# Four reading orders for the 512 tokens that stream through the paired gate and up products

## The chip, the core and the metric

The kernel runs on one core of a Trainium2 chip. The metric is device time in microseconds (us), the median over runs; for one execution there is also a hardware profile. Engines: TensorE (PE, with its weight loads shown as PEld), VectorE (DVE), ScalarE (ACT), GpSimd (POOL), and SyncE (SP), whose queue issues the transfers.

## The reference

One transformer block on 2048 tokens of width 448: sliding-window attention, then a gated feed-forward part, each after a layer norm and with a residual. The change is in the feed-forward part.

```python
def _B_ref(x, w_gate, w_up, w_down):
    g = jnp.einsum("bsd,df->bsf", x, w_gate)      # 448 -> 1792
    u = jnp.einsum("bsd,df->bsf", x, w_up)        # 448 -> 1792
    h = _gelu(g) * u
    return jnp.einsum("bsf,fd->bsd", h, w_down)   # 1792 -> 448
...
h = x + _A_ref(_layernorm(x, axis=-1), A_wqkv, A_wo)
h2 = h + _B_ref(_layernorm(h, axis=-1), B_w_gate, B_w_up, B_w_down)
```

All tensors are float32.

## The kernel before, in words

Every float32 operand of the large products is kept as a high and a low part, and each product is a sum of matmuls over pairs of parts (the list `TERMS`, 11 of them for the width of 448). `xT` holds the normalised activations transposed: partitions are the width, and the 2048 tokens lie one after another along the free axis.

The feed-forward part is cut into 56 products, numbered `n`. One product takes 128 of the 1792 hidden columns for one chunk `c` of 512 tokens: `g` and `u` of size 128 x 512 in two PSUM banks, then Gelu of `g` times `u`, then the down product, which adds to four banks of 128 tokens x 448. Products 0 to 3 are computed with all 128 rows of the array. Products from `PAIRED = 4` on are *paired*: a matmul over 128 rows is split into two over 64 rows each, issued one after the other by the helper `pair` (line 903 of the profile) with the tile positions 0 and 64; one of them adds to the bank of `g` while the other adds to the bank of `u`. In a first phase (10 pairs) the upper half serves `g`, in a second (11 pairs) the halves are swapped. The moving operand of each is `xT[HALF[x], xb, toks]`, 512 tokens of one chunk; for the last term of the upper half it is a copy in `rec[2]` (named `xh`).

The bank pair of a product is fixed by the parity of `n`, so the product after next writes the same banks. The order on PE is written out by hand at the end of `feed_forward`: first phase of product m, first half of the down product of m - 2, second phase of product m, second half of the down product of m - 2. All other engines' instructions are placed by a list scheduler (`Lists.run`) that goes by estimated costs, which the change leaves as they are.

After a product, five instructions turn its banks into the operand of the down product: the Gelu on ACT (line 965) reads the first bank through `src(0)` and writes `g2`; the multiply on DVE (line 967) reads the second bank through `src(1)` and `g2`; ACT makes the high part and DVE the low part (lines 328 and 331); the tiny copies of line 909 only mark that a bank has been finished. At the end of a group of products, line 998 adds the four banks of the down product to the residual `hres`, and in the last group line 1001 sends it out. The last product's down product is issued unpaired at line 992.

Of the kernel before, what the change touches and what calls it, by code (L numbers as in the profile page):

```python
# [11 lines left out]
AF = mybir.ActivationFunctionType  # L12
OP = mybir.AluOpType
# [39 lines left out]
PAIRED = 4  # L53
# [11 lines left out]
def mm(n):  # L65
    return max(n / 2400 + 0.0155, 0.115)
# [154 lines left out]
def block_kernel(ctx: ExitStack, tc, x, wqk_in, wv_in, wo_in, ffn_in, out):  # L221
    nc = tc.nc
# [3 lines left out]
    op = L.op  # L226
# [38 lines left out]
    bank = [psum.tile([128, 512], F32, name=f"bank{i}") for i in range(8)]  # L265
# [32 lines left out]
    def span(name, lo, n):  # L298
        return (name, lo, lo + n)
# [21 lines left out]
    def HR(t):  # L321
        return span("h", t, 1)
# [4 lines left out]
    def to_hi(dst, src):  # L327
        nc.scalar.activation(dst, src, AF.Copy)  # L328

    def to_lo(dst, src, hi, eng=None):  # L330
        (eng or nc.vector).tensor_sub(dst, src, f(hi))  # L331

    def dma(key, size, fn, r=(), w=(), cost=0.44, after=()):
        return op("sp", cost, 0, key, fn, r, w, size=size, after=after)
# [473 lines left out]
    def blocks(m):  # L808
        return m.rearrange("p (b n) -> p b n", b=4)
# [86 lines left out]
    down_a, down_b, phase, whole = {}, {}, {}, []  # L896
    HALF = (slice(0, 64), slice(64, 128))

    def pair(key, n, lat, a, b, r, banks):

        def go():
            for x, (bk, w, m, start, stop) in enumerate((a(), b())):
                nc.tensor.matmul(bank[bk.k][:, 0:n], w, m, start=bool(start), stop=bool(stop),  # L903
                                 tile_position=(64 * x, 0), skip_group_check=True)
        return op("pe", mm(n), lat, key, go, r, (), banks)

    def seen(key, b):

        op("act", 0.08, 0.17, key, lambda: nc.scalar.activation(word[0:1, 0:1], bank[b.k][0:1, 0:1], AF.Copy), (),  # L909
           (), b)  # L910

    def product(n, i, c, k, gn, gi, down):
        get, rat, _ = RECS[i % NR]
        key = FFN + 30 * n
        toks = slice(c * 512, (c + 1) * 512)
        early = n < EARLY
        paired = n >= PAIRED
        bs = []
        for q in range(0 if paired else 2):

            turn = 2 * (n - EARLY) + q + (2 if n == 2 else -2)
            b = Bank("early") if early else Bank(("ffn", turn))
            if not early:
                row[turn] = b
            bs.append(b)
            for a, (h, wb, xb) in enumerate(TERMS):
                whole.append(op("pe", mm(512), 0.403, key + (SWAP if n == 3 else 0) + q * NP + a / NP, lambda a=a, h=h, wb=wb, xb=xb, q=q, b=b: nc.tensor.matmul(  # L927
                    bank[b.k], get()[0][q][h][:, wb, :], xT[:, xb, toks], start=(a == 0), stop=(a == NP - 1)),
                   [span("xT", 4 * c, 4), *rat[q][h]], (), b, tag="early" if early else None))
        if paired:  # L930
            bs = [Bank(("fix", 2 * ((n + 1) % 2) + q)) for q in range(2)]
            phase[n] = [[], []]
            for ph in range(2):


                todo = TERMS if ph else TERMS[:-1]
                for a, (h, wb, xb) in enumerate(todo):
                    def side(x, a=a, h=h, wb=wb, xb=xb, ph=ph, todo=todo):
                        q = x ^ ph
                        m = rec[2][64:128, toks] if x and a == NP - 1 else xT[HALF[x], xb, toks]  # L940
                        return (bs[q], get()[0][q][h][HALF[x], wb, :], m, not ph and a == 0, ph and a == len(todo) - 1)
                    need = [span("xT", 4 * c, 4), *rat[0][h], *rat[1][h]] + ([("xh", c)] if a == NP - 1 else [])
                    phase[n][ph].append(pair(key + 11 * ph + a / NP, 512, 0.403, lambda side=side: side(0),
                                             lambda side=side: side(1), need, bs))
                if not ph:
                    seen(key + 11, bs[1])
        raw = [v_m[:, 1024 * n + 512 * q:1024 * n + 512 * q + 512] for q in range(2 * early)]
        held = [[span("vm", 1024 * n + 512 * q, 512)] if early else [] for q in range(2)]
        for q, b in enumerate(bs if early else ()):
            op("act", 0.49, 0.605, 16 * NB - 20, lambda q=q, b=b: nc.scalar.activation(raw[q], bank[b.k], AF.Copy), (),  # L950
               held[q], b)
        bs = [None, None] if early else bs
        m, o = GH[n % 2]
        at = [span("proj", o + 512 * h, 512) for h in range(2)]

        def gh(h):
            return blocks(m[:, o + 512 * h:o + 512 * h + 512])

        def src(q):
            return blocks(raw[q] if early else bank[bs[q].k])  # L960


        g2, G2 = (raw[0], held[0]) if early else (ge, ["ge"])
        table = 0 if n else 1.29
        op("act", 0.485 + table, 0.608 + table, key + NP, lambda: nc.scalar.activation(  # L965
            blocks(g2), src(0), AF.Gelu_apprx_tanh), held[0], G2, bs[0], after=exps)
        op("dve", 0.605, 0.702, key + 2 * NP, lambda: nc.vector.tensor_tensor(  # L967
            blocks(g2), src(1), blocks(g2), op=OP.mult), [*G2, *held[1]], G2, bs[1], port=early)
        op("act", 0.52, 0.635, key + 2 * NP, lambda: to_hi(gh(0), blocks(g2)), G2, [at[0]])
        op("dve", 0.6, 0.7, key + 2 * NP, lambda: to_lo(gh(1), blocks(g2), gh(0)), [*G2, at[0]], [at[1]], port=True)  # L970

        down_a[n], down_b[n] = [], []
        PARTS = ((0, 0), (1, 0), (0, 1))
        last = n == 4 * NF - 1
        for ph in range(0 if last else 2):
            for j in range(2):
                for a, (oh, wh) in enumerate(PARTS):
                    def side(x, a=a, oh=oh, wh=wh, ph=ph, j=j):  # L980
                        q = 2 * j + (x ^ ph ^ k % 2)
                        return (down[q], gh(oh)[HALF[x], q, :], get()[0][2][wh][HALF[x]], not ph and k == 0 and a == 0,
                                ph and k == gn - 1 and a == 2)
                    (down_b if ph else down_a)[n].append(pair(
                        key + 2 * NP + 6 * ph + 3 * j + a, D, 0.38, lambda side=side: side(0), lambda side=side: side(1),
                        [at[oh], *rat[2][wh]], [down[2 * j], down[2 * j + 1]]))
                if not ph:
                    seen(key + 2 * NP + 3 * j + 3, down[2 * j + 1 - k % 2])

        for a, q in ((0, 0), (0, 1), (2, 0), (2, 1), (1, 0), (1, 1), *((a, q) for q in (2, 3) for a in range(3))) if last else ():  # L990
            oh, wh = PARTS[a]
            down_b[n].append(op("pe", mm(D), 0.38, key + 2 * NP + 3 * q + a, lambda a=a, oh=oh, wh=wh, q=q: nc.tensor.matmul(
                bank[down[q].k][:, 0:D], gh(oh)[:, q, :], get()[0][2][wh], start=False, stop=(a == (1 if q < 2 else 2)),
                skip_group_check=True), [at[oh], *rat[2][wh]], (), down[q]))
        if k == gn - 1:
            for q in range(4):
                t = 4 * c + q
                op("dve", 0.533, 0.626, key + 2 * NP + 3 * q + 3, lambda t=t, b=down[q]: nc.vector.tensor_tensor(  # L998
                    hres[:, t, :], bank[b.k][:, 0:D], hres[:, t, :], op=OP.add), [HR(t)], [HR(t)], down[q])
                if gi == len(GROUPS) - 1:  # L1000
                    dma(key + 40, 224, lambda t=t: nc.sync.dma_start(outr[t * 128:(t + 1) * 128, :], hres[:, t, :]),
                        [HR(t)], ())


    exps = []
# [148 lines left out]
```

## Time and profile before

| what | value |
|---|---|
| median of 2 runs | 734.53 us (734.46 to 734.6) |
| the profiled execution's own time | 734.23 us |
| its span, first to last instruction | 732.5 us |
| mean granted TensorE clock | 0.999 |
| PE busy | 723.8 us (99%) |
| DVE, ACT, POOL busy | 395.9, 365.8, 160.3 us |
| chain that ended last, by engine | PE 93%, ACT 2%, DVE 2%, DMA 1% |

A profile describes one execution; the shares of the chain tell where the end of the run was decided, the busy shares only how full an engine was. A row of the groups reads: line, engine, operation, output from inputs, shape and count, then busy us and mean ns of one, then the engine's idle time before such instructions and what ended it. Matmuls are pipelined, so the mean ns of one matmul is longer than the distance from one start to the next.

### The profile page before, as it was taken

The numbers are of one execution on the slowest core, as the hardware profiler recorded it, in microseconds if no ns is written. First come the engines' busy times: TensorE is split into PE (matmuls) and PEld (weight loads), VectorE is DVE, ScalarE is ACT, GpSimd is POOL, SyncE is SP. The second block draws the span as 40 slices with busy tenths as digits, with TensorE's granted clock in tenths as the row PEclk, the third lists the DMA queues.
The fourth block names the chain that finished last, engine by engine and source line by source line (L and its number), as shares of the span: only waits on it lengthen the run. The fifth ranks groups of instructions, "written<-read, shape, count | busy, mean of one in ns | idle before, by whom it ended". The sixth has DMA issues, their size and how long they took to land.

```text
span 732.5 us, 15381 instructions
## 1 busy us (share of the span) xinstructions
PE 723.8 (99%) x5893; PEld 604.6 (83%) x5893; DVE 395.9 (54%) x1057; ACT 365.8 (50%) x930; POOL 160.3 (22%) x253
## 2 busy tenths in 40 slices
PE   8999999999999999999999999999999999999997
PEld 7887888788888787768888888888888888888886
DVE  7977876776677788748554223144223243233223
ACT  7668776667666888876553222243222233222221
POOL 5615343343344547462000000000000000000000
PEclk9999999999999999999999999999999999999999
DMA  8888445755565777514652000012100000001012
GB/s 285 260 280 248 146 148 179 202 178 156 162 201 160 191 229 206 147 36 102 153 174 88 1 2 1 1 43 84 43 1 2 1 1 2 1 1 52 11 42 101
DMA packets 83138, 79.12 MB, mean 108 GB/s; under 512 B 34104, under 2 KB 72952, under 8 KB 83064
## 3 DMA queue, kind: packets, MB, share of 16 engines
q1 hardware_dynamic: 83064, 78.14, 35.3%
q8 instruction: 46, 0.75, 0.4%
q14 instruction: 28, 0.23, 0.1%
HBM read 48.23 MB, written 29.36 MB: 106 GB/s over the span
## 4 chain that ended last, share of the span: by engine, by line
PE 93%; ACT 2%; DVE 2%; DMA 1%; issue 1%; POOL 0%; SPq 0%; DVEq 0%; ACTq 0%; POOLq 0%
PE bank L903 52%; PE bank L580 9%; PE bank L701 6%; PE bank L629 6%; PE bank L735 6%; PE bank L535 5%; PE bank L779 5%; PE bank L927 2%; PE bank L383 1%; ACT pp L705 1%; DVE mt L633 1%; ACT xT L328 0%; DVE hres L782 0%; DMA hres<-in_x_dram 0%; PE bank L660 0%
## 5 line engine op out<-in xcount | busy, mean ns | idle before, releaser
L633 DVE CUSTOM_DVE_ANT_0 mt<-bank,mt 128x384 bf16<-128x384 f32 (+2 forms) x256 | 127.5, 524 | 38.2 <-PE bank L629 36.4
L705 ACT ACTIVATE pp<-bank 128x384 f32<-128x384 f32 (+2 forms) x352 | 121.5, 388 | 52.4 <-PE bank L701 46.5
L967 DVE TENSOR_TENSOR mt<-bank,mt 128x512 f32<-128x512 f32 x54 | 37.1, 688 | 139.5 <-ACT mt L965 139.5
L716 POOL TENSOR_SCALAR_AFFINE_SELECT pp<-pp 128x512 f32<-128x512 f32 x120 | 75.5, 642 | 124.8 <-ACT pp L705 115.0
L580 PE MATMUL bank<-xT,proj 128*128 128x512 f32 x308 | 101.2, 402 | 0.0
L701 PE MATMUL bank<-rq,rk 104*128 104x384 f32 (+2 forms) x352 | 96.8, 305 | 0.9 <-ACT pp L705 0.6
L965 ACT ACTIVATE mt<-bank 128x512 f32<-128x512 f32 x54 | 32.2, 596 | 113.5 <-PE bank L903 113.5
L629 PE MATMUL bank<-rk,rq 84*128 84x384 f32 (+2 forms) x256 | 82.7, 344 | 0.1
L903 PE MATMUL bank<-xT,rec 64*128 64x512 f32 x656 | 82.0, 388 | 0.0
L903 PE MATMUL bank<-xT,rk 64*128 64x512 f32 x656 | 82.0, 388 | 0.0
L701 PEld LDWEIGHTS bank<-rq,rk 104*128 104x128 f32 x352 | 64.7, 189 | 19.3 <-ACT pp L705 4.8
L903 PEld LDWEIGHTS bank<-xT,rec 64*128 64x128 f32 x656 | 63.0, 184 | 12.2
L903 PEld LDWEIGHTS bank<-xT,rk 64*128 64x128 f32 x656 | 63.0, 184 | 12.2
L998 DVE TENSOR_TENSOR hres<-bank,hres 128x448 f32<-128x448 f32 x64 | 35.5, 616 | 66.1 <-PE bank L903 63.9
L328 ACT ACTIVATE proj<-mt 128x512 fp32r<-128x512 f32 x54 | 34.1, 631 | 71.8 <-DVE mt L967 52.5
L903 PE MATMUL bank<-xT,proj 64*128 64x512 f32 x533 | 66.7, 388 | 0.0
L909 ACT ACTIVATE word<-bank 1x1 f32<-1x1 f32 x162 | 25.6, 158 | 79.2 <-PE bank L903 78.6
L580 PEld LDWEIGHTS bank<-xT,proj 128*128 128x128 f32 x308 | 55.9, 190 | 6.0 <-issue 0.8
L535 PE MATMUL bank<-proj,xT 128*128 128x224 f32 x352 | 60.2, 278 | 0.1
L903 PEld LDWEIGHTS bank<-xT,proj 64*128 64x128 f32 x533 | 51.1, 184 | 10.1 <-ACT word L909 0.3
L331 DVE TENSOR_TENSOR proj<-mt,proj 128x512 fp32r<-128x512 f32 x54 | 37.3, 691 | 36.8 <-ACT proj L328 28.5
L535 PEld LDWEIGHTS bank<-proj,xT 128*128 128x128 f32 x352 | 53.0, 191 | 1.8 <-DVE hres L782 0.3
(117 smaller groups left out, 1106.6 us busy)
## 6 DMA issues: line engine op xcount, KB each, us to landing
rk<-k SPq DMA_DIRECT2D x44, 336.0 KB
rq<-q SPq DMA_DIRECT2D x32, 336.0 KB
q<-proj SPq DMA_DIRECT2D x15, 448.0 KB
raw<-in_ffn_dram SPq DMA_DIRECT2D x7, 736.0 KB
v<-in_ffn_dram SPq DMA_DIRECT2D x7, 736.0 KB
k<-proj SPq DMA_DIRECT2D x11, 448.0 KB
hres<-in_x_dram SPq DMA_DIRECT2D x16, 224.0 KB
out_dram<-hres SPq DMA_DIRECT2D x16, 224.0 KB
```

The lines of the kernel that those rows point to most:

```text
L331: (eng or nc.vector).tensor_sub(dst, src, f(hi))
L535: op("pe", mm(224), 0.29, key + a / 16, lambda a=a, h=h, wb=wb, xb=xb: nc.tensor.matmul(bank[b.k][:, 0:224], xT[:, xb, t * 128:(t + 1) * 1 ...
L580: op("pe", mm(512) + 0.002, 0.403, key, lambda a=a, h=h, wb=wb, xb=xb: nc.tensor.matmul(bank[b.k], wqk[i][:, h, wb, :], xT[:, xb, c * 512: ...
L629: nc.tensor.matmul(bank[b.k][:, o:384], rq[u][0:3 * DH, j, i * 128:i * 128 + 128], rk[u][0:3 * DH, j, m0 * 128:(i + 3) * 128], start=True, ...
L633: nc.vector.tensor_tensor_reduce(junk[s % 2][:, o:384], bank[b.k][:, o:384], mask[:, o:384], 1.0, -BIG, OP.add, OP.max, mx[i // 2][:, i % ...
L701: nc.tensor.matmul(bank[b.k][:, 0:n], rk[u][0:104, j, m * 128:m * 128 + 128], rq[u][0:104, j, lo * 128:(hi + 1) * 128], start=True, stop=True)
L705: nc.scalar.activation(pp[:, j, o * 128:o * 128 + n], bank[b.k][:, 0:n], AF.Exp, scale=SCALE)
L716: nc.gpsimd.affine_select(a, a, pattern=[[0, 4], [-cm, 128]], compare_op=op_, fill=0.0, base=0, channel_multiplier=cm)
L735: nc.tensor.matmul(bank[b.k][32 * j:32 * j + DH + 1, lo * 128:(hi + 1) * 128], v[:, 4 * c - 2 + m, g % 2, j, :], pp[:, j, at[m] * 128:(at[ ...
L779: op("pe", mm(D), 0.38, wk, lambda a=a, h=h, oh=oh, wh=wh, i=i, k=k: nc.tensor.matmul(bank[k.k][:, 0:D], ohl[:, h, oh, i * 128:(i + 1) * 1 ...
L903: nc.tensor.matmul(bank[bk.k][:, 0:n], w, m, start=bool(start), stop=bool(stop), tile_position=(64 * x, 0), skip_group_check=True)
L967: op("dve", 0.605, 0.702, key + 2 * NP, lambda: nc.vector.tensor_tensor(blocks(g2), src(1), blocks(g2), op=OP.mult), [*G2, *held[1]], G2, ...
```

## The change

For the paired products, the 512 tokens are read in an order that depends on `n % 4`. Order 0 is the stored one. Order 1 takes tokens 0, 256, 1, 257 and so on. Order 2 takes tokens 0, 32, 64 to 480, then 1, 33 and so on. Order 3 takes 16 tokens from the first half, 16 from the second, and so on. Output columns are still written to the bank one after another, so the columns of a bank stand in the order in which the tokens were read. The Gelu and the multiply read the bank with the inverse order, so that `g2` and all that follows have the tokens in their usual places. With order 1 their reads of the bank have a step of 2 elements, with order 2 a step of 16, with order 3 they go by runs of 16. Products 0 to 3 and the down products are as before.

```diff
+    READ = [None, ("p (h t) -> p t h", dict(h=2)), ("p (h t) -> p t h", dict(h=16)),
+            ("p (h k l) -> p k h l", dict(h=2, l=16))]
+    BACKW = [("p (b t) -> p b t", dict(b=4)), ("p (t h) -> p h t", dict(h=2)), ("p (t h) -> p h t", dict(h=16)),
+             ("p (k h l) -> p h k l", dict(h=2, l=16))]
+    PLAIN = [("p (b t) -> p b t", dict(b=4)), ("p (h t) -> p h t", dict(h=2)), ("p (h t) -> p h t", dict(h=16)),
+             ("p (h k l) -> p h k l", dict(h=2, l=16))]
+    SAME = [None, ("p (t h) -> p t h", dict(h=2)), ("p (t h) -> p t h", dict(h=16)),
+            ("p (k h l) -> p k h l", dict(h=2, l=16))]
+    def seen_as(ap, how):
+        return ap if how is None else ap.rearrange(how[0], **how[1])
-    def pair(key, n, lat, a, b, r, banks):
+    def pair(key, n, lat, a, b, r, banks, order=None):
         def go():
             for x, (bk, w, m, start, stop) in enumerate((a(), b())):
-                nc.tensor.matmul(bank[bk.k][:, 0:n], w, m, start=bool(start), stop=bool(stop),
+                o = bank[bk.k][:, 0:n]
+                if order is not None:
+                    o, m = seen_as(o, SAME[order]), seen_as(m, READ[order])
+                nc.tensor.matmul(o, w, m, start=bool(start), stop=bool(stop),
                                  tile_position=(64 * x, 0), skip_group_check=True)
...
+        way = n % 4 if n >= PAIRED else 0
...
-                                             lambda side=side: side(1), need, bs))
+                                             lambda side=side: side(1), need, bs, way))
...
-            return blocks(raw[q] if early else bank[bs[q].k])
+            return seen_as(raw[q] if early else bank[bs[q].k], BACKW[way])
...
-            blocks(g2), src(0), AF.Gelu_apprx_tanh), held[0], G2, bs[0], after=exps)
+            seen_as(g2, PLAIN[way]), src(0), AF.Gelu_apprx_tanh), held[0], G2, bs[0], after=exps)
...
-            blocks(g2), src(1), blocks(g2), op=OP.mult), [*G2, *held[1]], G2, bs[1], port=early)
+            seen_as(g2, PLAIN[way]), src(1), seen_as(g2, PLAIN[way]), op=OP.mult), [*G2, *held[1]], G2, bs[1], port=early)
```

## The prediction

> **What bounds the kernel now.** I read the head of the page first, then the chain of waits, then what TensorE (PE) waited for.
>
> ```profile
> span 732.5 us, 15381 instructions
> PE 723.8 (99%) x5893; PEld 604.6 (83%) x5893; DVE 395.9 (54%) x1057; ACT 365.8 (50%) x930; POOL 160.3 (22%) x253
> PEclk9999999999999999999999999999999999999999
> PE bank L903 52%; PE bank L580 9%; PE bank L701 6%; PE bank L629 6%; PE bank L735 6%; PE bank L535 5%; PE bank L779 5%; PE bank L927 2%; PE bank L383 1%; ACT pp L705 1%; DVE mt L633 1%; ACT xT L328 0%; DVE hres L782 0%; DMA hres<-in_x_dram 0%; PE bank L660 0%
> 346.57 379.30 PE bank L903 x3462
> PE bank L903 <- ACT word L909: 0.2, 1, 0.2
> ```
>
> PE is busy for 99% of the span at full granted clock, so there is no clock to win. Line 903 is the helper `pair`, which issues every paired matmul. From 346.57 us the chain lies on it for 379.30 us without a break, and the last row says that in the whole run it waited once, for 0.2 us, on another engine. So in the second half of the kernel a nanosecond added to a paired matmul is a nanosecond of the end. This is the half that the change touches.
>
> Next, how much of it the change touches. The groups by shape give the matmuls of the gate and up products: 64 rows by 512 tokens.
>
> ```profile
> L903 PE MATMUL bank<-xT,rec 64*128 64x512 f32 x656 | 82.0, 388 | 0.0
> L903 PE MATMUL bank<-xT,rk 64*128 64x512 f32 x656 | 82.0, 388 | 0.0
> L903 PE MATMUL bank<-xT,proj 64*128 64x512 f32 x533 | 66.7, 388 | 0.0
> L903 PE MATMUL bank<-xT,rq 64*128 64x512 f32 x287 | 35.9, 388 | 0.0
> L903 PE MATMUL bank<-xh,rk 64*128 64x512 f32 x16 | 6.2, 386 | 0.0
> L903 PE MATMUL bank<-xh,rec 64*128 64x512 f32 x16 | 6.2, 386 | 0.0
> L903 PE MATMUL bank<-xh,proj 64*128 64x512 f32 x13 | 5.0, 386 | 0.0
> L903 PE MATMUL bank<-xh,rq 64*128 64x512 f32 x7 | 2.7, 386 | 0.0
> ```
>
> The counts add up to 2184 matmuls, that is 1092 pairs; at 10 + 11 = 21 pairs for each product these are the 52 paired products, numbers 4 to 55. Thirteen products fall to each of the four orders, or 273 pairs. The mean of 388 ns is a latency that overlaps its neighbours. What a pair costs the path is read from starts, in one product of the timeline (start us, length us):
>
> ```profile
> 600.39 2.45 PE L903 MATMUL bank<-xT,rk 64*128 64x512 f32 x20
> 602.68 1.38 PE L903 MATMUL bank<-proj 64*128 64x448 f32 x12
> 603.89 2.67 PE L903 MATMUL bank<-xT,rk 64*128 64x512 f32 x21
> ...
> 606.40 1.37 PE L903 MATMUL bank<-proj 64*128 64x448 f32 x12
> 606.61 0.60 ACT L965 ACTIVATE mt<-bank 128x512 f32<-128x512 f32 x1 [2.29 <-PE bank L903]
> 607.24 0.69 DVE L967 TENSOR_TENSOR mt<-bank,mt 128x512 f32<-128x512 f32 x1 [3.35 <-ACT mt L965]
> ...
> 607.62 0.62 PE L903 MATMUL bank<-xT,proj 64*128 64x512 f32 x4
> ```
>
> Ten pairs of 512 tokens take 602.68 - 600.39 = 2.29 us and eleven take 606.40 - 603.89 = 2.51 us: 4.80 / 21 = 229 ns a pair. Twelve pairs of 448 columns take 1.21 + 1.22 = 2.43 us: 202.5 ns a pair. The difference, 26 ns for 64 columns, is 0.41 ns per column. So of the 229 ns some 209 ns (512 x 0.41) are the streaming of tokens, and 20 ns are fixed. The whole product takes 607.62 - 600.39 = 7.23 us.
>
> **The change part by part.** Nothing is removed and no instruction is added: the built kernel has the same instructions on every engine in the same order, apart from one DVE multiply that gains a wait on an earlier instruction of its own engine. DVE works in order and that multiply has the slack shown below, so I price this at 0.
>
> What is different are access patterns, in three places.
>
> *1. The tokens that stream into PE.* Order 0 is the present one. In order 1 neighbours in the stream lie 256 tokens apart (1024 bytes), in order 2 they lie 32 apart (128 bytes), in order 3 the stream has runs of 16 tokens in a row (64 bytes). No PE row of this trace has such a stream; every moving operand of it is read in a row. So the price is bounded by the nearest rows of other engines.
>
> ```profile
> L705 ACT ACTIVATE pp<-bank 128x256 f32<-128x256 f32 x112 | 39.5, 382 | 16.6 <-PE bank L701 13.5 <-PE bank L735 1.6 <-POOL pp L716 0.6
> L705 ACT ACTIVATE pp<-bank 128x128 f32<-128x128 f32 x112 | 26.4, 277 | 20.2 <-PE bank L701 19.6
> L328 ACT ACTIVATE v<-bank 128x224 f32<-128x224 f32 x32 | 11.4, 356 | 2.6 <-PE bank L535 2.3
> L491 POOL MEMSET mt<- 128x384 f32 x1 | 0.4, 423 | 0.1
> L464 POOL MEMSET ident<- 128x128 f32 x1 | 0.2, 204 | 0.1
> L486 POOL MEMSET v<- 128x128 f32 x1 | 0.3, 335 | 0.0
> ```
>
> Runs: the third row writes `v` in runs of 28 with a gap of one after each. By the two rows above it an element costs (382 - 277) / 128 = 0.82 ns, so 224 in a row would take 277 + 96 x 0.82 = 356 ns: what it takes. Runs cost nothing there, and I price order 3 at 0. Single elements: the last row fills the ones' column of `v`, 128 elements that lie 29 apart (116 bytes). The two memsets above it give (423 - 204) / 256 = 0.86 ns per element in a row, with 95 ns fixed; scattered it is (335 - 95) / 128 = 1.88 ns. A lone element costs 2.2 times one in a row, 1.02 ns more. Spans on this engine are rough and it writes where PE reads, so this bounds rather than tells.
>
> The lower bound for orders 1 and 2 is 0: one engine's address generator needn't say anything of another's. A gain has no source, since the stream is already what PE is bound by. Upward the row can be carried over in three ways: as a ratio (209 ns of streaming about doubles, +209 to +249 ns a pair), as an addition (+1.02 ns x 512 = +522 ns), or as a rate (512 x 1.88 + 20 - 229 = +754 ns). I take the ratio at a round two, one scattered token in the time of two: a row of an engine with another clock lends its ratio more safely than its nanoseconds. That is 2 orders x 273 pairs x 0.209 us = 114.1 us, all on the path, as the chain shows. The two matmuls of a pair read different partitions and run side by side, so a pair pays once.
>
> [...]
>
> *2. The evictions.* The Gelu (line 965) and the multiply (line 967) read the banks with a step of 2 elements in order 1, of 16 in order 2, in runs of 16 in order 3, so that the tokens come out in place. Between 0 and the 0.52 us of the scattered price (512 x 1.02 ns) each, 1.04 us together. The cover: in the timeline they end at 607.24 + 0.69 = 607.93 us, and their two banks are next written by the product after next, at 607.62 + 7.23 = 614.85 us. 6.9 us of slack hide 1.04 us, so 0. With that cover gone it would be 26 x 1.04 = 27 us.
>
> *3. The tail.* The last product, 55, has order 3, and its chain has less cover:
>
> ```profile
> 722.86 0.69 DVE L967 TENSOR_TENSOR mt<-bank,mt 128x512 f32<-128x512 f32 x1 [2.98 <-ACT mt L965]
> ...
> 724.32 0.69 DVE L331 TENSOR_TENSOR proj<-mt,proj 128x512 fp32r<-128x512 f32 x1 [0.76 <-ACT word L909]
> ...
> 725.80 2.33 PEld L992 LDWEIGHTS bank<-rec,proj 128*128 128x128 f32 x12 [0.30 <-issue]
> ```
>
> The last split ends at 724.32 + 0.69 = 725.01 us, 0.79 us before the last down product begins. Runs cost 0 as above; at the full 1.04 us the end would move by 0.25 us.
>
> The sum, on the profiled execution's own time of 734.2 us (span 732.5 and 1.7 around it; the median of the runs is 0.3 above it, which is nothing beside the terms): 734.2 + 114.1 + 0 + 0 = **848 us**.
>
> **The rivals.**
>
> *The order is free for PE.* [...] For it: the runs of 28 cost ACT nothing, and the weight loads run under the matmuls unharmed, so the memory side has room. Against it: the memset row. Then only the tail's 0 to 0.25 us remain: 734 us, not slower. [...]
>
> [...]
>
> *It pays more than double.* At the additive price 546 x 0.522 = 285 us: 1019 us; at the rate of 1.88 ns 546 x 0.754 = 412 us: 1146 us. [...] Against it: one rough row of 335 ns carries it.
>
> *Faster.* I find only chance: a shift of the schedule can't come from unchanged lists.
>
> **How the numbers follow.** Doubling on orders 1 and 2: 0.32, with its own range of 840 to 875 us (the ratios 2.0 to 2.2 and the evictions). Free: 0.29. Half or part: 0.15. More than double: 0.23. Faster: 0.01. A change of about 2% can be told from none here. All paying cases are beyond that: slower 0.70, same 0.29, faster 0.01. The range has to reach down to the free case, 731 us, and up to the additive price, 1020 us; the rest of the dear case, some 0.11, is left out.
>
> **What would show it.** Right: in the stretches of orders 1 and 2 the starts of pairs lie about 440 ns apart and a product takes about 11.6 us (7.23 + 21 x 0.209), while those of orders 0 and 3 keep 229 ns and 7.2 us; PE is still 99% busy at full clock and the chain is still on the paired matmuls. Wrong in size: a slot other than 440 ns, or one that differs between orders 1 and 2. Wrong in kind: 229 ns throughout, or PE idle behind a Gelu or a multiply longer than 1.2 us. Order 3 above 229 ns would make the reading of runs wrong.

## The result, and the profile after

791.53 us against 734.53 us: the ratio is 1.0776, 95% interval 1.073 to 1.0822. The profiled execution took 791.6 us, its span is 57.4 us longer. First the head of the page, then one row of the chain of waits and two of what PE waited for:

```profile
span 789.9 us, 15382 instructions
PE 779.9 (99%) x5893; PEld 610.3 (77%) x5893; DVE 395.9 (50%) x1057; ACT 366.3 (46%) x930; POOL 159.9 (20%) x253
PEclk9999999999999999999999999999999999999999
346.71 436.55 PE bank L920 x3462
PE bank L383 <- ACT xn L378: 1.2, 2, 0.6
PE bank L920 <- ACT word L926: 0.2, 1, 0.2
```

`pair` is now line 920. The same 3462 paired matmuls start 0.14 us later (346.71 us for 346.57) and take 436.55 us in place of 379.30: 57.3 us, so the whole loss lies here. PE is still full, the clock still whole, and the paired matmuls still wait once for another engine, for 0.2 us. The wait of line 383 was 0.2 us before; it falls in the first 8 us, and no more than the 0.14 us of it reaches the paired matmuls. The timeline of products 5 to 8 tells which order it is (start us, length us; product 5 has order 1, 6 order 2, 7 order 3, 8 the stored order 0):

```profile
354.68 2.32 PE L920 MATMUL bank<-xT,rq 64*128 64x512 f32 x20
356.84 1.39 PE L920 MATMUL bank<-proj 64*128 64x448 f32 x12
...
361.65 4.51 PE L920 MATMUL bank<-xT,proj 64*128 64x512 f32 x20
365.98 1.42 PE L920 MATMUL bank<-proj 64*128 64x448 f32 x12
...
373.25 2.56 PE L920 MATMUL bank<-xT,proj 64*128 64x512 f32 x20
375.65 1.40 PE L920 MATMUL bank<-rq,proj 64*128 64x448 f32 x12
...
380.75 2.46 PE L920 MATMUL bank<-xT,rq 64*128 64x512 f32 x20
383.04 1.38 PE L920 MATMUL bank<-proj 64*128 64x448 f32 x12
```

Ten pairs take 2.16, 4.33, 2.40 and 2.29 us: **order 1: 216 ns a pair, order 2: 433, order 3: 240, stored: 229**. Order 1, whose neighbours lie 1024 bytes apart, is *faster* than the stored order. Taken this way for each of the 52 products, the values of one order differ by at most 3 ns, and the eleven pairs of the second phase agree with them within 3 ns.

The evictions did not notice. The Gelu and the multiply, over all their instructions, before (lines 965 and 967) and after (duration ns min/median/max):

```profile
L965 ACT ACTIVATE mt<-bank x54: 572/597/598, 337.0 to 722.2; 128x512 f32<-128x512 f32 x54
L967 DVE TENSOR_TENSOR mt<-bank,mt x54: 677/691/692, 341.9 to 722.9; 128x512 f32<-128x512 f32 x54
L983 ACT ACTIVATE mt<-bank x54: 571/597/599, 337.1 to 779.6; 128x512 f32<-128x512 f32 x54
L985 DVE TENSOR_TENSOR mt<-bank,mt x54: 678/691/693, 342.1 to 780.3; 128x512 f32<-128x512 f32 x54
```

The medians are the same 597 and 691 ns. Reading a bank with a step of 2 or 16 elements, or by runs of 16, costs ACT and DVE nothing here.

### The profile page after: what moved, and what is told of

Read it like the earlier page. It is cut to its first block, busy times and chain, and to the rows that moved or that the text cites. A ratio compares the mean times of both kernels' runs of the same rounds, so it can differ in the third digit from the quotient of the medians.

```text
span 789.9 us, 15382 instructions
## 1 busy us (share of the span) xinstructions
PE 779.9 (99%) x5893; PEld 610.3 (77%) x5893; DVE 395.9 (50%) x1057; ACT 366.3 (46%) x930; POOL 159.9 (20%) x253
## 4 chain that ended last, share of the span: by engine, by line
PE 90%; DVE 4%; ACT 3%; DMA 1%; issue 1%; POOL 1%; DVEq 0%; SPq 0%; ACTq 0%; POOLq 0%
PE bank L920 56%; PE bank L580 8%; PE bank L701 5%; PE bank L629 5%; PE bank L735 5%; PE bank L535 4%; PE bank L779 4%; PE bank L945 2%; DVE mt L633 1%; ACT pp L705 1%; PE bank L383 1%; DMA raw<-in_wqk_dram 1%; DVE hres L782 1%; ACT rq L328 1%; ACT xT L328 1%
## 5 line engine op out<-in xcount | busy, mean ns | idle before, releaser
L920 PE MATMUL bank<-xT,rec 64*128 64x512 f32 x656 | 108.9, 474 | 0.0
L920 PEld LDWEIGHTS bank<-xT,rec 64*128 64x128 f32 x656 | 65.2, 191 | 32.0 <-issue 23.4
L920 PE MATMUL bank<-xT,rk 64*128 64x512 f32 x656 | 86.2, 402 | 0.0
L920 PE MATMUL bank<-xT,proj 64*128 64x512 f32 x533 | 74.2, 419 | 0.0
```

Source lines behind the costliest of these rows:

```text
L920: nc.tensor.matmul(o, w, m, start=bool(start), stop=bool(stop), tile_position=(64 * x, 0), skip_group_check=True)
```

## The experiments

Since the price is read per product, one kernel can hold eight orders (`way = n % 8`) and one profile prices them all. The prices are in ns a pair, taken from the first phase (ten pairs) of the kernel's products and good to 1 or 2 ns. The second phase (eleven pairs) gives the same within 3 ns, but for three orders that are named below. Each kernel with eight orders ran once, so its prices are compared within that run. The edits below change the lists `READ`, `BACKW`, `PLAIN` and `SAME` together; only `READ` is shown.

### Undoing order 2

```diff
-            ("p (h t) -> p t h", dict(h=2)), ("p (h t) -> p t h", dict(h=16)),
+            ("p (h t) -> p t h", dict(h=2)), None,
```

> The change with its order 2 undone: products with number 2 modulo 4 read the stored order, orders 1 and 3 stay. If order 2 alone makes the loss (273 pairs x 203 ns = 55.5 us), the rest is orders 1 and 3: 734.4 + 273 x (11.1 - 13.3) ns = 733.8 us, and with the down pairs' small excess at most 736 us. Rival (the three orders disturb one another or the evictions cost something too): 740 us or more.

735.59 us, ratio 1.0007 (0.9997 to 1.0016) against the kernel before: no difference. The pairs take 229, 216, 230 and 240 ns. Order 2 is the whole loss; what order 3 costs, order 1 brings back.

### Two places, seven distances

```diff
+    READ = [None, ("p (a h t) -> p a t h", dict(h=2, t=4)), ... t=8, 16, 32, 64, 128 ...,
+            ("p (h t) -> p t h", dict(h=2))]
```

> Products cycle through eight orders (by the product's number modulo 8): the stored one, and seven in which two places of the row are read in turn, token by token, that lie 4, 8, 16, 32, 64, 128 or 256 tokens apart (16 to 1024 bytes). Always two places, only the distance changes. Theory L (a few lines already fetched are kept, the number of interleaved places decides): all seven at 215 to 217 ns a pair like order 1, stored at 229 ns; total about 734.5 - 7/8 x 1092 x 13.3 ns = 722 us. Theory B (neighbours in the stream must not fall in the same part of the memory, the distance alone decides): 32 tokens apart costs what order 2 cost, 433 ns, 256 apart 216 ns, and every distance in between is one or the other; total about 751 us with one order at 433 ns and 29.5 us more for each further one. Theory D (any lone token costs double and order 1 is an exception of its own): six at 433 ns, about 899 us.

Its product 4 reads two places that lie 32 tokens apart, the distance of order 2:

```profile
347.56 2.32 PE L943 MATMUL bank<-xT,proj 64*128 64x512 f32 x20
349.72 1.40 PE L943 MATMUL bank<-rq,proj 64*128 64x448 f32 x12
```

2.16 us, 216 ns. So it is for all seven distances (216), the stored order takes 229; 723.92 us in all, where theory L said 722. Theories B and D are out: order 2's distance isn't what costs. Of theory L this run bears out the prices alone: that lines are fetched and kept was its author's supposition, which no run shows.

### More places

```diff
+    READ = [None, ("p (h t) -> p t h", dict(h=4)), ... h=8, 16, 32, 64, 128, 256]
```

> Eight orders again: the stored one, and 4, 8, 16, 32, 64, 128 or 256 evenly spaced places read in turn (512, 256, 128, 64, 32, 16 and 8 bytes apart). [...] Theory B: the price follows the distance: the 512- and 256-byte ones take what the same distances (128 and 64 tokens) take with two places. Total 790 to 900 us.

| places | 1 (stored) | 4 | 8 | 16 | 32 | 64 | 128 | 256 |
|---|---|---|---|---|---|---|---|---|
| ns a pair | 229 | 281 | 488 | 432 | 431 | 430 | 459 | 451 |

928.04 us. The last column is the telling one; these are product 7's rows:

```profile
382.74 4.69 PE L943 MATMUL bank<-xT,proj 64*128 64x512 f32 x20
387.25 1.41 PE L943 MATMUL bank<-rq,proj 64*128 64x448 f32 x12
```

4.51 us for ten. Its stream is 0, 2, 4, 6, ...: it walks along the row by 8 bytes a token, without a jump but one back, and takes 451 ns. Nor does the price keep rising with the number of places: 8 cost 488 ns, 16 to 64 some 431. So how many places are read in turn does not give the price by itself either. The time was above the 790 to 900 us that were expected.

### Runs from two halves

```diff
+    READ = [None, ("p (h k l) -> p k h l", dict(h=2, l=2)), ... l=4, 8, 16, 32, 64, 128]
```

> Eight orders: the stored one, and runs of 2, 4, 8, 16, 32, 64 or 128 tokens taken in turn from the first and the second half. Known: runs of 1 take 216 ns, runs of 16 take 240 ns, the stored order 229 ns. Theory S (each change of place costs a fixed time, 11 ns for 31 changes): 0.36 ns a change, so 231, 234 and 229 + 23 = 252 ns at runs of 64, 32 and 8, 275 at 4, 321 at 2. [...]

| run length | 2 | 4 | 8 | 16 | 32 | 64 | 128 | 512 (stored) |
|---|---|---|---|---|---|---|---|---|
| ns a pair | 339 | 251 | 243 | 240 | 237 | 229 | 229 | 229 |

Product 9 has runs of 2, here with both of its phases:

```profile
384.27 3.57 PE L943 MATMUL bank<-xT,proj 64*128 64x512 f32 x20
387.66 1.39 PE L943 MATMUL bank<-proj 64*128 64x448 f32 x12
388.89 3.83 PE L943 MATMUL bank<-xT,proj 64*128 64x512 f32 x21
...
392.56 1.38 PE L943 MATMUL bank<-proj 64*128 64x448 f32 x12
```

Ten pairs take 3.39 us, 339 ns each; the eleven of the second phase 3.67 us, 333 or 334 ns each. 756.21 us in all. Theory S doesn't hold: it named 321 and 252 ns for runs of 2 and 8 (339, 243), but 275 for runs of 4 (251). Runs of 1 take 216 and runs of 2 take 339, though both alternate between the same two halves. What differs is the parity: with runs of 1 *every other* token of the stream walks through one half in a row; with runs of 2 it jumps from half to half.

### Every other token

This led to theory E: the price goes as if the even and the odd places of the stream were read apart, so what counts is how far *every other* token lies from the next of its kind. In the stored order that is 8 bytes (229 ns), with two halves in turn 4 (216), in the walk 0, 2, 4, 6, ... 16 (451), in order 2 more (433). So E expects order 2's price, taken as 432, where each such step is 16 bytes or more, and the price of the stored order or of the runs from two halves (251 ns for runs of 4, 243 for 8) where at least every second step is 8 bytes or less. It is an estimate from these prices. The edit names patterns for which the theories part:

```diff
+    READ = [None,
+            ("p (h m l) -> p l m h", dict(h=2, l=2)),   # 0, 256, 2, 258, ...; then l=4 and l=8
+            ...
+            ("p (a h t) -> p a t h", dict(h=2, t=2)),   # 0, 2, 1, 3, 4, 6, ...
+            ("p (m j l) -> p j m l", dict(m=16, l=2)),  # 0, 1, 32, 33, ...; then l=4 and l=8
+            ...]
```

> Eight orders by the product's number modulo 8 that tell apart who reads what. [...] Rival P (a pattern whose innermost count is two distinct places is cheap by its form): all three two-half orders stay at 216 ns. Total by E about 734.5 + 136.5 x (3 x 0.203 + 0.021 + 0.014) = 822 us, by P some 735 us.

| stream | steps of every other token, bytes | E said | measured |
|---|---|---|---|
| 0, 256, 2, 258, ... | 8 | 226 to 240 | 229 |
| 0, 256, 4, 260, ... | 16 | 432 | 451 |
| 0, 256, 8, 264, ... | 32 | 432 | 460 |
| 0, 2, 1, 3, 4, 6, ... | 4, 12 | 229 | 230 |
| runs of 2, 16 places | 128 | 432 | 449 |
| runs of 4, 16 places | 8, 120 | 250 | 246 |
| runs of 8, 16 places | 8, 8, 8, 104 | 243 | 222 |

The rows of products 9 (first line of the table), 10 (second) and 13 (fifth):

```profile
395.48 2.53 PE L943 MATMUL bank<-xT,proj 64*128 64x512 f32 x20
397.77 1.46 PE L943 MATMUL bank<-proj 64*128 64x448 f32 x12
...
402.71 4.75 PE L943 MATMUL bank<-xT,proj 64*128 64x512 f32 x20
407.20 1.49 PE L943 MATMUL bank<-rq,proj 64*128 64x448 f32 x12
...
434.03 4.76 PE L943 MATMUL bank<-xT,rk 64*128 64x512 f32 x20
438.51 1.50 PE L943 MATMUL bank<-rq,proj 64*128 64x448 f32 x12
```

2.29, 4.49 and 4.48 us. The first two are patterns of one form, both alternate between the halves, and differ in the step inside a half alone: 229 ns at 8 bytes, 451 at 16. The third reads two neighbours one after the other each time, and pays the full price (449); so two neighbours in a row are not enough. Rival P fails: its 216 ns came for none of the two-half orders. Six of seven fall near where E put them (the paying ones 4 to 6.5% above its 432). Runs of 8 came out below, and their two phases differ; product 15:

```profile
453.59 2.46 PE L943 MATMUL bank<-xT,rec 64*128 64x512 f32 x20
455.81 1.46 PE L943 MATMUL bank<-rk,proj 64*128 64x448 f32 x12
457.03 2.61 PE L943 MATMUL bank<-xT,rec 64*128 64x512 f32 x20
...
459.62 1.46 PE L943 MATMUL bank<-rk,proj 64*128 64x448 f32 x12
```

2.22 us for ten pairs and 2.59 us for eleven: 222 and 235 ns, 229 over all 21. So the order alone doesn't fix the price of a pair; what else does is not shown. The whole kernel took 834.67 us, where E said 822; of that 3.2 us are two waits for `xT` early on:

```profile
360.77 2.20 PE L943 MATMUL bank<-xT,rq 64*128 64x512 f32 x8 [2.59 <-DMA xT<-xn]
```

From about 392 us, some products after these waits, until 762 us the second matmul of a pair starts some 83 ns after the first, where in the other runs it is 3 to 4. The granted clock was 0.93 in the mean from 330 to 400 us and 1.00 from there to 750 us. So small differences of this run against the others are less certain than large ones.

### Seams

> What a seam between runs costs. Eight orders: stored; runs of 16 tokens from 4, 8 or 16 places in turn (places 128, 64, 32 tokens apart); runs of 8 from 4, 8 or 32 places (128, 64, 16 apart); runs of 32 from 4 places. [...] Theory F (a seam costs a fixed time): all runs of 16 take 240 ns, of 8 243 ns, of 32 237 ns, as the alternating halves did. [...]

Runs of 16 from 4, 8 and 16 places take 234, 238 and 240 ns, runs of 8 from 4, 8 and 32 places 231, 264 and 233, runs of 32 from 4 places 234; 744.86 us. In the second phase runs of 8 from 8 places take 253 ns. Runs of one length differ by up to 33 ns with the spacing (27 over all 21 pairs), so theory F is out. None lies below 229, and no rule by distance shows. What order 3's 11 ns are made of stays open.

### Two places everywhere

If the 13 ns that two places gained (216 for 229) are to be had wherever the stored order is read, every long matmul should gain. Four kernels, each with more of them on `READ[1]`, banks read back in order:

```diff
-        way = n % 4 if n >= PAIRED else 0
+        way = 1 if n >= PAIRED else 0
```

> All 52 paired products read two halves in turn (order 1), none another order. If the 13.3 ns a pair that order 1 gained are its own and not borrowed from the neighbouring products, 1092 x 13.3 ns = 14.5 us are gained: 734.5 - 14.5 = 720 us, 2.0% below the kernel before, and the stretches show 216 ns throughout. Rival: the gain is given back in the down products or in a wait for the Gelu or the multiply, whose cover shrinks from 7.23 to 6.95 us a product: then 730 us or more, with waits of PE on ACT or DVE in the profile.

723.12 us, ratio 0.9836 (0.9819 to 0.9852). The pairs take 216 ns nearly throughout (all but one of the 104 phases lie between 215 and 219), and the mean length of one matmul on `xT` and `rec` falls from 388 to 376 ns. 12.1 of 14.5 us arrive, a gain of 1.6%. Part of the rest is a wait of PE early on, 1.7 us in two waits of which 1.5 us are one; before there was one of 0.2 us:

```profile
PE bank L919 <- ACT word L925: 1.7, 2, 1.5
...
366.10 4.88 DMA xT<-xn
```

The row below it, of the chain, says what is late: the transposed tokens of a later chunk, which PE now reaches sooner.

> All paired products and all down products stream two halves in turn (down: 448 output columns as two halves of 224; the adds to the residual read the banks back in order). Theory E: the stored order uses a reader's whole line rate, so each matmul starts with a stumble of some 13 to 16 ns that two halves avoid, whatever the length: a down pair falls from 203 to 187 + 2.4 = 189 ns; 660 x 14 = 9 us below the run with the gate and up products alone (723.1), so 714 us. Rival (the 13 ns is a matter of 512 tokens, i.e. of filling a whole bank, or of the gate and up operand): down pairs stay at 203 ns and the time at 723 us.

715.23 us, 0.9737 (0.9722 to 0.9751). A down half in the timeline, 6 pairs:

```profile
505.18 1.30 PE L919 MATMUL bank<-rk,proj 64*128 64x448 f32 x12
506.31 1.89 PE L919 MATMUL bank<-xT,rec 64*128 64x512 f32 x16
```

1.13 us, 188 ns for 448 columns (189 in the median of all down halves), where it was 202.5: the gain is 13 ns whether 512 or 448 are streamed. So it is a fixed loss of each matmul, as E said; that it falls at the matmul's start is not shown, nor is the rate of a reader that E gave as its reason.

> As the run before, and also the matmuls over 128 rows with 224 to 512 columns: the projections (308 of 512), products 0 to 3 (88 of 512), values (352 of 224), output projection (192 of 448) and the last down product (12 of 448). In the kernel before, their distances in a row are 231 to 233, 203 and 111 ns, that is 15 to 18 ns over the streaming at 0.417 ns a column. Theory E: all lose 13 to 15 ns: 952 x 14 ns = 13 us at most, about 700 us if all of it lies on the path; in the attention half PE also waits for other engines, so part may be lost: 700 to 710 us. Rival (the stumble comes from two matmuls sharing the array as a pair): no change from the run before.

710.79 us, 0.9677 (0.966 to 0.9693), just above the range. The same stretch of unpaired matmuls, first in the kernel before and then here:

```profile
331.82 3.81 PE L927 MATMUL bank<-xT,rq 128*128 128x512 f32 x16
335.47 5.03 PE L779 MATMUL bank<-wos,ohl 128*128 128x448 f32 x24
340.33 1.55 PE L927 MATMUL bank<-xT,rq 128*128 128x512 f32 x6
...
327.28 3.62 PE L944 MATMUL bank<-xT,rq 128*128 128x512 f32 x16
330.73 4.70 PE L791 MATMUL bank<-wos,ohl 128*128 128x448 f32 x24
335.27 1.46 PE L944 MATMUL bank<-xT,rq 128*128 128x512 f32 x6
```

Sixteen of 512 columns take 3.65 us before and 3.45 here, 228 and 216 ns each; 24 of 448 columns of the output projection take 4.86 and 4.54 us, 202.5 and 189. They are unpaired, so the pair is not the cause of this loss. For the 512-column projections, which run among other work, the median from start to start falls from 233 to 217 ns, and the mean length of one from 402 to 388. The 224-column values stay at 111 ns (mean length 278 and 276); what bounds them is not shown.

> As the run before, and also scores and probabilities (384, 256 or 128 columns). Their 384-column matmuls now lie some 18 ns over the streaming; 128-column ones are bound by something else. Theory E gives about 350 x 14 ns = 5 us less of PE time; but in this half the chain also runs over ACT and DVE, so 0 to 5 us less than the run before. Rival: the strided reads of the banks slow the maxima on DVE or the exponentials on ACT, which then bound this half: slower than the run before.

708.40 us, 0.9657 (0.9628 to 0.9685): 26 us below the kernel before, and 2.4 us below the last kernel, inside the 0 to 5 us that were expected. In the kernel before, the matmuls of 384 columns lay 179 ns from start to start in the median, those of 128 columns in a row (line 701) 62; what bounds the latter is not shown. The page of this run:

```profile
span 706.9 us, 15386 instructions
PE 694.2 (98%) x5893; PEld 601.7 (85%) x5893; DVE 395.2 (56%) x1057; ACT 363.2 (51%) x930; POOL 159.7 (23%) x253
```

PE does the same 5893 matmuls in 29.6 us less; the maxima and exponentials read their banks in halves without loss (ACT 363.2, DVE 395.2 us busy).

## Why the prediction was right or wrong

*The sign and the path: right.* A slower kernel was forecast with 0.70, because paired matmuls are the path without cover. The 57.3 us lie on them and nowhere else. The time lies in the stated range of 731 to 1020 us, but that range was drawn to hold both the free and the dear case. The forecast of 848 us and the 840 to 875 us of its own case were missed.

*The term of order 2: right.* 273 x 209 ns = 57 us was said; 273 x 204 = 55.7 us came (433 - 229). In this order a scattered token does take the time of two.

*The term of order 1: wrong, and it is the step that failed.* The prediction gave it the same +209 ns; it measured -13. That is 57 + 3.5 = 61 us of the 848 forecast. "A gain has no source" failed with it. The gain comes out of the 20 ns of a pair that the prediction took as fixed: with two places, 215.8 ns for 512 columns and 189.2 for 448, a column costs 0.416 ns and the fixed part is 3 ns. A doubling on order 2 alone, to which "half or part" with its 0.15 comes nearest, gives 734 + 57 = 791 us, and 791.53 came, partly by luck, since the gain of order 1, the loss of order 3 and the 2.0 us of a term below nearly cancel. Most prices go by how far *every other* token steps: 229 ns at 8 bytes, 451 at 16.

*Order 3: wrong by a little.* Runs were priced at 0 by the row of ACT; they cost 273 x 11 ns = 3.0 us. A row that shows another engine *writing* runs says little of PE reading them.

*The evictions and the tail: right at 0,* even below the argument: their price was bounded at 0.52 us each and hidden, and the medians of both did not move by 1 ns.

*A term that was left out:* the down pairs that follow a phase of order 1, 2 or 3 take 205, 210 and 205 ns in the mean for 202, some 156 pairs each, 2.0 us together; why is not shown. The sum as measured: 55.7 - 3.5 + 3.0 + 2.0 = 57.2 us for a span that grew by 57.4.

*The choice of the ratio* (2.2 on the fill of `v`, taken as 2) over the addition and the rate was borne out for order 2: no order of the 35 that were priced beside the stored one cost 522 or 754 ns more; the dearest, 8 places, cost 259 ns more. That a rough row of POOL, which writes, gave the ratio of PE's reads is luck all the same: the one ratio was to hold for both orders and held for one. The clock of POOL, the reason given for the ratio, is shown by no run; what the rows show is its pace, 0.86 ns an element in a row for 0.41 ns a column on PE.

Theory E is a model that the prices fit, not something that was seen. It leaves open why 4 places (281) and runs of 2 from two halves (339) cost less than 432, although every other token of theirs steps by 1016 bytes or more, and 8 places (488) more. It also leaves open why one order takes 222 ns in one phase and 235 in the other. That a down pair takes 187 + 2.4 ns, as it was worked out for one of the runs, no run shows as a sum of these two; measured are 189 ns, of which 3 are fixed by the estimate above. The orders that pay were run on pairs alone, so whether an unpaired matmul would pay as much is not shown.

## What to carry to other kernels

Where PE is the bound and streams float32 operands, look at the order in which the columns are read: two places read in turn cost nothing to write, the banks can be read back in order for free, and here the matmuls of 448 and 512 columns became 12 to 16 ns shorter each (202.5 to 189, 228 to 216 and 233 to 217 ns), and the kernel 3.4% in all. Streams in which every other token steps by 16 bytes or more each time took 281 to 488 ns in place of 229, most of them about double. When the price of an access pattern is unknown, put several patterns into one kernel and read them off one profile, rather than carry a row over from another engine.

## What the runs showed of the hardware that was not expected

- A stream of two alternating places is faster than a contiguous one: 216 against 229 ns for 512 columns, at each of seven distances from 16 to 1024 bytes, and 189 against 202 for 448.
- A step of 8 bytes from token to token is enough to double the price: 0, 2, 4, 6, ... takes 451 ns for 229.
- ACT and DVE read PSUM with steps of 2 and 16 elements at the speed of contiguous reads (medians of 597 and 691 ns, before and after).
- In one run the two matmuls of a pair went on some 83 ns apart for 370 us, from some products after two waits, and the stored order still took 226 to 229 ns from pair to pair.
